# Groups of 512 tokens instead of 256 in a fused lightning-attention and MLP kernel

## The chip, the cores and the metric

The kernel runs on one core of a Trainium2 chip. Times are device microseconds. A kernel's reported time is the median of several executions; a profile is taken of one of these executions (for the kernel before, of one more), and its span is 1.7 to 1.9 us shorter than the time of that execution (2.3 us in e10). The kernel before takes 732.7 us.

The engines are called as the profile does: PE is TensorE (PEld its weight loads), DVE is VectorE, ACT is ScalarE, POOL is GpSimd, SP issues the loads and stores.

## The reference

Attention with decay over 64-token blocks, then an MLP with leaky ReLU:

```python
# q, k, v: (4, 8, 768, 64) float32; lam: (8,)
for b in range(nb):                                  # per block, per head
    intra = einsum('bhic,bhjc->bhij', qb, kb) * Dmask
    intra = einsum('bhij,bhjd->bhid', intra, vb)
    inter = einsum('bhid,bhde->bhie', qb * lam_pow, kv_state)
    out[:, :, sl] = intra + inter
    kv_state = lam_block * kv_state + einsum('bhsd,bhse->bhde', kb * rev_pow, vb)
x = out.transpose(0, 2, 1, 3).reshape(3072, 512)
h = x @ w_in                                         # 512 -> 2048, weights stored as float64
g = maximum(0.01 * h, h)
return g @ w_out                                     # 2048 -> 512
```

The kernel handles attention in 24 chunks of 128 tokens, one "step" of the program per chunk.

## The kernel before

Three parts matter: the products, the conversion of the weights, and the schedule.

**Products.** Each matrix product is done with seven block products instead of eight. Operands are quadrants A11 to A22 and sums of them, S1 to S4; the weights have B11 to B22 and differences T1 to T4. The seven products of a unit run in the order P1, P2, P6, P5, P7, P3, P4, into two kinds of PSUM bank: Z (two of them) and W (one). P6, P7 and P4 add onto Z, where P1 left its result, so P1's result has to be copied out ("keep 0") before P6 may add onto it:

```python
return [lambda: (mult("Z", "P1", ins("P1"), True), keep(0, "Z")),
        lambda: (mult("W", "P2", ["tot1"] + ins("P2"), True), total(0, "W")),
        lambda: (mult("Z", "P6", ["keep0"] + ins("P6")), keep(1, "Z")),
        lambda: (mult("W", "P5", ["tot0"] + ins("P5"), True), keep(3, "W")),
        ...]
```

`keep` is a copy of a product's result on ScalarE, except in a down unit (the second matrix product) that adds to an earlier unit's result. There it is an addition into the output tile `os` on VectorE. An up unit (the first matrix product) ends with the sums S1, S2, S3 of its results on VectorE, which the down unit needs, and the down unit adds S4 after P2. The sums of the attention's output x (tile `xs`) run on POOL:

```python
for o, a, b, op in (("S1", "A21", "A22", ALU.add), ("S2", "S1", "A11", ALU.subtract),
                    ("S3", "A11", "A21", ALU.subtract), ("S4", "A12", "S2", ALU.subtract)):
    if o in names:
        e = nc.vector if eng == "DVE" else nc.gpsimd
        run(eng, us, lambda: e.tensor_tensor(t[o], t[a], t[b], op=op), after, ("sum", eng, o))
```

A group is 256 tokens, so a quadrant holds C = 128 tokens. A unit holds UP = 4 pairs of feature blocks:

```python
# up                                                  # down
for i in range(UP):                                   for i in range(UP):
    for kk in range(2):                                   nc.tensor.matmul(t, lhsT=G[..][:, i*C:(i+1)*C],
        nc.tensor.matmul(t[:, i*C:(i+1)*C],                   rhs=WO[UP*u + i][:, SO[sb], :], ...)
            lhsT=w[:, kk, :], rhs=x[:, kk, :], ...)
```

**Conversion.** A weight block arrives as float64 words and is made float32 by three ScalarE instructions and, on VectorE, a clamp, a shift and an integer addition of 512 columns each. After two blocks of a pair, four differences T1 to T4 run on POOL.

**Schedule.** The program emits instructions in an order found with its own clocks per engine: nine attention steps first, then units with one attention step in most up units.

## Time and profile before

| | kernel before |
|---|---|
| reported time | 732.7 us |
| span of the profiled execution | 731.2 us |
| TensorE busy | 709.6 us |
| first up product starts | 59.0 us |
| TensorE idle before it, after it | 17.4 us, 4.2 us |

The page and the order of time are read in the prediction. One view more, each engine's busy time in a stretch, splits the span at the first product. The columns are: stretch, its length, busy us (and instructions) of PE, PEld, DVE, ACT and POOL, the granted clock, the DMA share, GB/s.

```profile
0.00:58.99 58.99, 41.56 (x536) 34.78 (x537) 45.19 (x71) 38.06 (x62) 38.49 (x47) 0.97 0.96 250
58.99:731.20 672.21, 667.99 (x5098) 617.61 (x5096) 242.34 (x396) 184.12 (x323) 121.66 (x138) 1.00 0.15 42
```

Length less PE's busy time is idle TensorE time: 17.4 us ahead of the first product, 4.2 us in all the rest.

### The profile page before, as it was taken

The page shows a single profiled execution, that of the slowest core. Times are in us where ns is not written, and L with a number is a line of the kernel's source. Part 1 is how long each engine was busy: PE and PEld are TensorE (multiplying, and loading weights), DVE is VectorE, ACT ScalarE, POOL GpSimd, SP SyncE. Part 2 cuts the span into 40 slices and gives each one's busy share as a digit, 9 for nine tenths or more (in the row PEclk, how much of TensorE's full clock was granted, in tenths as well). Part 3 has the DMA queues.
Part 4 walks back from the last instruction along what each step waited for, and adds up shares of the span by engine and source line. Part 5 has one row for each costly group of instructions (what it writes and reads, how often), then busy time and mean ns, then how long its engine had stood idle before and what let it go on. Part 6 is the DMA issues. An engine that isn't in the chain of part 4 may idle for free.

```text
span 731.2 us, 12969 instructions
## 1 busy us (share of the span) xinstructions
PE 709.6 (97%) x5632; PEld 652.4 (89%) x5632; DVE 287.5 (39%) x466; ACT 222.2 (30%) x385; POOL 160.2 (22%) x184
## 2 busy tenths in 40 slices
PE   5779999999999999999999999999999999999998
PEld 4668988999999999989999999899899899999997
DVE  5888996724313223222321332321321323123213
ACT  4777875611312222123022131121122122111211
POOL 2879766513103102003011110200100001001000
PEclk9999999999999999999999999999999999999999
DMA  8999635302111011110210200000000000000000
GB/s 217 268 256 268 203 108 168 87 30 58 29 30 45 30 44 44 44 30 13 62 45 1 73 1 1 2 30 1 12 18 1 30 1 1 30 1 0 30 1 29
DMA packets 89289, 42.78 MB, mean 59 GB/s; under 512 B 75920, under 2 KB 84112, under 8 KB 89232
## 3 DMA queue, kind: packets, MB, share of 16 engines
q1 hardware_dynamic: 89088, 41.95, 20.8%
q8 instruction: 44, 0.72, 0.4%
q14 instruction: 13, 0.11, 0.0%
q10 hardware_dynamic: 144, 0.00, 0.0%
HBM read 35.66 MB, written 6.29 MB: 57 GB/s over the span
## 4 chain that ended last, share of the span: by engine, by line
PE 92%; DVE 4%; ACT 2%; issue 1%; DMA 1%; SPq 0%; DVEq 0%; ACTq 0%
PE Z L502 24%; PE Z L527 22%; PE W L502 18%; PE W L527 16%; PE ps L352 3%; PE pt L328 3%; PE po L415 3%; PE po L372 2%; PE pu L401 2%; DVE gS L476 1%; DMA k<-in_k_dram 1%; DVE sc L358 1%; DVE wi L278 0%; DVE wo L283 0%; DVE wi L274 0%
## 5 line engine op out<-in xcount | busy, mean ns | idle before, releaser
L527 PE MATMUL Z<-wo,gA 128*128 128x256 f32 x552 | 131.9, 382 | 0.0
L527 PEld LDWEIGHTS Z<-wo,gA 128*128 128x128 f32 x552 | 103.0, 190 | 15.5 <-issue 2.4
L502 PE MATMUL W<-xs,wi 128*128 128x128 f32 x768 | 95.2, 277 | 0.0
L502 PE MATMUL Z<-x,wi 128*128 128x128 f32 x768 | 93.7, 275 | 0.0
L502 PE MATMUL Z<-xs,wi 128*128 128x128 f32 x768 | 93.7, 275 | 0.0
L502 PEld LDWEIGHTS Z<-x,wi 128*128 128x128 f32 x768 | 91.3, 192 | 1.5 <-issue 0.3
L502 PEld LDWEIGHTS W<-xs,wi 128*128 128x128 f32 x768 | 89.5, 192 | 2.0 <-issue 0.2
L502 PEld LDWEIGHTS Z<-xs,wi 128*128 128x128 f32 x768 | 89.6, 192 | 0.1
L527 PE MATMUL W<-wo,gA 128*128 128x256 f32 x368 | 86.9, 379 | 0.0
L455 DVE TENSOR_TENSOR gA<-gA,W 128x512 f32<-128x512 f32 x46 | 31.7, 688 | 129.8 <-PE W L502 129.8
L451 ACT COPY gA<-Z 128x512 f32<-128x512 f32 x46 | 27.0, 586 | 173.0 <-PE Z L502 173.0
L527 PEld LDWEIGHTS W<-wo,gA 128*128 128x128 f32 x368 | 69.8, 190 | 9.5
L467 ACT ACTIVATE gA<-gA 128x512 f32<-128x512 f32 x69 | 43.4, 629 | 112.2 <-DVE gA L455 112.1
L381 POOL TENSOR_TENSOR k<-k,decay 128x512 f32<-128x512 f32 x20 | 23.3, 1163 | 210.2 <-PE pt L328 210.2
L476 POOL TENSOR_TENSOR xs<-x 128x256 f32<-128x256 f32 x28 | 23.3, 831 | 191.5 <-PE W L502 191.5
L502 PE MATMUL W<-x,wi 128*128 128x128 f32 x384 | 46.8, 275 | 0.0
L455 DVE TENSOR_TENSOR gA<-gA,Z 128x512 f32<-128x512 f32 x23 | 15.8, 688 | 76.2 <-PE Z L502 76.2
L502 PEld LDWEIGHTS W<-x,wi 128*128 128x128 f32 x384 | 44.8, 192 | 0.0
L527 PE MATMUL Z<-wo,gS 128*128 128x256 f32 x184 | 44.0, 382 | 0.3
L527 PE MATMUL W<-wo,gS 128*128 128x256 f32 x184 | 43.6, 380 | 0.0
L358 DVE TENSOR_TENSOR sc<-ps,decay 128x512 f32<-128x512 f32 x48 | 30.9, 685 | 31.3 <-PE ps L352 31.3
L527 PEld LDWEIGHTS Z<-wo,gS 128*128 128x128 f32 x184 | 34.5, 190 | 6.8 <-DVE os L449 1.9
(77 smaller groups left out, 782.6 us busy)
## 6 DMA issues: line engine op xcount, KB each, us to landing
ws<-in_moe_w_in_dram SPq DMA_DIRECT2D x16, 512.0 KB, 5.5
ws<-in_moe_w_out_dram SPq DMA_DIRECT2D x16, 512.0 KB, 4.8
k<-in_k_dram SPq DMA_DIRECT2D x24, 256.0 KB, 4.0
q<-in_q_dram SPq DMA_DIRECT2D x24, 256.0 KB, 4.4
v<-in_v_dram SPq DMA_DIRECT2D x24, 256.0 KB, 4.6
out_dram<-os SPq DMA_DIRECT2D x24, 256.0 KB, 2.0
lam_b<-in_lam_dram ACTq DMA_DIRECT2D x1, 4.0 KB, 3.9
```

The lines of the kernel that those rows point to most:

```text
L328: nc.tensor.transpose(out=pt[:, hp, :], in_=pair(loaded[c][i], hp), identity=ident)
L352: nc.tensor.matmul(ps[hi][:, hp, :], lhsT=kT[b][HALF[hi], hp, :], rhs=qT[b][HALF[hi], hp, :], start=(hp == 0), stop=True, skip_group_check ...
L358: run("DVE", 0.72, lambda: nc.vector.tensor_tensor(sc[b][:, hi], ps[hi], decay[:, hi], op=ALU.mult), ["ps"], ("sc", b))
L372: nc.tensor.matmul(po[b][HALF[hi], hp, :], lhsT=state[(b - 1) % 2][HALF[hi], hp, :], rhs=qsT[b][HALF[hi], hp, :], start=(hp == 0), stop=False,
L381: run("POOL", 1.2, lambda: nc.gpsimd.tensor_tensor(kr, kr, _bc(pow_k, 3, D), op=ALU.mult), [("pt", "k")], ("kd", a))
L415: nc.tensor.matmul(po[b][HALF[hi], hp, :], lhsT=tv[:, 2 * hp + hi, :], rhs=sc[b][:, hi, hp, :], start=(not inter and hp == 0), stop=True, ...
L451: run("ACT", 0.6 if long else 0.38, lambda: nc.scalar.copy(dst(i), st[tag]), [tag], f"keep{i}")
L455: lambda: nc.vector.tensor_tensor(dst(i), dst(i), st[tag], op=ALU.add), [f"keep{i}", tag], f"tot{i}")
L467: run("ACT", 0.64, lambda: nc.scalar.activation(out=dst, in_=src, func=AF.Prelu, bias=0.0, scale=1.0, alpha=0.01), [after], gives)
L476: run(eng, us, lambda: e.tensor_tensor(t[o], t[a], t[b], op=op), after, ("sum", eng, o))
L502: nc.tensor.matmul(t[:, i * C:(i + 1) * C], lhsT=w[:, kk, :], rhs=x[:, kk, :], start=(first and i == 0 and kk == 0), stop=(i == UP - 1 and ...
L527: nc.tensor.matmul(t, lhsT=G[g, u][sa][:, i * C:(i + 1) * C], rhs=WO[UP * u + i][:, SO[sb], :], start=(first and i == 0), stop=(i == UP - ...
```

## The change

Its intent: matmuls that move 256 columns also in up products, a smaller first unit so that products start earlier, fewer and wider instructions on VectorE for the conversion, and some of the weights' differences on VectorE.

```diff
-    NG = NCH // 2
+    GC = 4
+    NG = NCH // GC
+    T = GC * C // 2          # 256 tokens in a quadrant
-    UP = 4
+    UP = 2
-    NX = 6
-    NF = 2
+    NX = 3
+    WARM = 10
...
+    idle = pp.tile([P, 2 * P], F32, name="idle", tag="W")
+    for _ in range(WARM):
+        nc.tensor.transpose(out=idle[:, 0:P], in_=ident, identity=ident)
...
+    T_DVE = [0, 3, 4, 6, 11, 13, 14]
+    FIRST, STEPS = 5, [1, 0, 0, 2, 2, 2, 1, 1, 0, 0, 1, 0, 0, 0, 0, 2]
...
         def clamp():
-            nc.vector.tensor_scalar(dest(), dest(), HI_MIN, HI_MAX, op0=ALU.max, op1=ALU.min)
+            d = W[p][:, 0:4, :].rearrange("p a b -> p (a b)")      # 1024 columns; the shift too
+            nc.vector.tensor_scalar(d, d, HI_MIN, HI_MAX, op0=ALU.max, op1=ALU.min)
...
-            for o, x, y in (("T1", "B12", "B11"), ("T2", "B22", "T1"), ("T3", "B22", "B12"), ("T4", "B21", "T2")):
-                later["POOL"].append((yes, 0.9, part(o, x, y), [("w", n)], (o, n)))
+        eng, e = ("DVE", nc.vector) if n // 2 in T_DVE else ("POOL", nc.gpsimd)
+        for o, x, y, m in (("T1", "B12", "B11", 2), ("T2", "B22", "T1", 1), ("T4", "B21", "T2", 1)):
+            ...                                                    # T1 and T3 in one, m = 2
...
-                sums("POOL", 0.8, ...x quadrants..., A[4:], [("x", 2 * g + 1)])
+                sums("DVE" if g == 0 else "POOL", ..., A[4:], [("x", GC * g + GC - 1)])
...
# up
-                    nc.tensor.matmul(t[:, i * C:(i + 1) * C], lhsT=w[:, kk, :], rhs=x[:, kk, :],
+                    nc.tensor.matmul(t[:, i, :], lhsT=w[:, kk, :], rhs=x[:, kk, :],       # 256 columns
# down
-            for i in range(UP):
-                nc.tensor.matmul(t, lhsT=G[g, u][sa][:, i * C:(i + 1) * C], rhs=WO[...], ...)
+            for m in range(T // P):
+                for i in range(UP):
+                    nc.tensor.matmul(t[:, m, :], lhsT=G[g, u][sa][:, i, m * P:(m + 1) * P], rhs=WO[...], ...)
```

Cuts are marked by "...". Not shown are the new order of loads, the bookkeeping of staging rooms, and the output tile, which is now a whole group's and written in four parts.

More of the change, by code (lines that the diff above doesn't have):

```diff
@@ L78 @@
     NCH = B * NCB
-    NG = NCH // 2
+    GC = 4
+    NG = NCH // GC
+    T = GC * C // 2
     NP = FO // 2
     HD = d_model // 2
-    UP = 4
+    UP = 2
     NU = NP // UP
-    NX = 6
-    NF = 2
+    NX = 3
+    WARM = 10
     HALF = (slice(0, D), slice(D, 2 * D))
-    assert D == 64 and KO == HP == 4 and S % C == 0 and NCH % 2 == 0 and NP % UP == 0
+    assert D == 64 and KO == HP == 4 and S % C == 0 and NCH % GC == 0 and NP % UP == 0
     const = ctx.enter_context(tc.tile_pool(name="const", bufs=1))
@@ L140 @@
     NW = len(blocks)
-    ROOMS = [f"{w}{p}" for w in ("wi", "wo") for p in range(UP, NP)]
-    ROOMS[-2:-2] = ["st0", "st1"]
-    ROOMS_G = ROOMS[-2:]
-    LOADS = "wccwcwcwwcwccwwwwcwwcwwcwwcwwwwwwwwwwwwwwww" + "c" * NCH
-    SLACK, AHEAD = 0.4, 6.0
-    PLAN = [('a', 0, 0, 9), ('i', 0, 0, 1), ('i', 1, 0, 1), ('o', 0, 0, 1), ('o', 1, 0, 0)]
-    PLAN += [(w, g, u, w == "i") for g in range(NG) for u in range(g < NF, NU) for w in "io"]
-    busy = set(ROOMS_G)
+    ROOMS = ["st"] + [f"{w}{p}" for w, p, h in reversed(blocks) if h == 0 and p >= UP]
+    LOADS = "ccwwcwcccwcwwwwcwwwwwccwwwwwwcwwwwwwwwwwwww" + "c" * NCH
+    SLACK, AHEAD = 0.7, (8.0, 16.0)
+    T_DVE = [0, 3, 4, 6, 11, 13, 14]
+    FIRST, STEPS = 5, [1, 0, 0, 2, 2, 2, 1, 1, 0, 0, 1, 0, 0, 0, 0, 2]
     rooms = {}
@@ L197, in pump @@
     def pump(urgent=False):
-        while urgent or clk["DMA"] < clk["PE"] + AHEAD:
+        while urgent or clk["DMA"] < clk["PE"] + AHEAD[fin > 3]:
             able = [x for x in sorted(y[0] for y in loads.values() if y) if x[2]()]
@@ L208, in load_w @@
         rooms[n] = room_free(n)
-        pool, size = (tp, 2 * d_model) if rooms[n][:2] == "st" else (wop, 7 * QB)
+        pool, size = (tp, 2 * d_model) if rooms[n] == "st" else (wop, 7 * QB)
         t = pool.tile([P, size], F32, name="ws", tag=rooms[n], bufs=1)
@@ L217, in go, with taken, conversion @@
                 nc.sync.dma_start(out=w_raw[n], in_=moe_w_out[f * P:(f + 1) * P, :])
-        run("DMA", 1.95, go, [("w", m) for m in range(n) if rooms[m] == rooms[n]], ("raw", n))
+        run("DMA", 1.95, go, [("lowp", m) for m in range(n) if rooms[m] == rooms[n]], ("raw", n))
         ready["raw", n] += 2.0
     def room_free(n):
-        later_on = {f"{w}{p}" for w, p, h in blocks[n + 1:] if (w, p) != blocks[n][:2]} | {"st0", "st1"}
-        taken = busy.union(rooms[m] for m in range(w_done, n))
-        return next((r for r in ROOMS if r in later_on and r not in taken), None)
+        later_on = {f"{w}{p}" for w, p, h in blocks[n + 1:] if (w, p) != blocks[n][:2]} | {"st"}
+        return next((r for r in ROOMS if r in later_on and r not in taken()), None)
+    def taken():
+        return {rooms[m] for m in w_raw}
     HI_MAX = _float_of(0x47EFFFFF)
     HI_MIN = _float_of(0x38100000)
-    def conversion(n):
+    def conversion(n, first):
         kind, p, h = blocks[n]
@@ L250, in may @@
         def may():
-            tag = f"{kind}{p}"
-            return n <= w_done + 2 and tag not in busy and all(rooms[m] != tag for m in range(w_done, len(rooms)))
+            return h == 1 or n <= w_done + 2 and f"{kind}{p}" not in taken()
         def magnitude():
@@ L271, in sign_part @@
             nc.scalar.activation(out=addend(BF16, 1), in_=words(1, F32), func=AF.Sign, bias=tiny[:, 0:1])
+            del w_raw[n]
         def clamp():
-            nc.vector.tensor_scalar(dest(), dest(), HI_MIN, HI_MAX, op0=ALU.max, op1=ALU.min)
+            d = W[p][:, 0:4, :].rearrange("p a b -> p (a b)")
+            nc.vector.tensor_scalar(d, d, HI_MIN, HI_MAX, op0=ALU.max, op1=ALU.min)
         def shift():
-            d = dest().bitcast(I32)
+            d = W[p][:, 0:4, :].rearrange("p a b -> p (a b)").bitcast(I32)
             nc.vector.tensor_scalar(d, d, 3, None, op0=ALU.logical_shift_left)
@@ L283, in low @@
             nc.vector.tensor_tensor(d, d, lo.pop(n).rearrange("p (a b) -> p a b", a=2), op=ALU.add)
-            del w_raw[n]
             w_done = n + 1
@@ L288, in yes, with part @@
             return True
-        def part(out, a, b):
-            return lambda: nc.gpsimd.tensor_tensor(W[p][:, s[out], :], W[p][:, s[a], :], W[p][:, s[b], :], op=ALU.subtract)
-        later["ACT"].append((may, 0.69, magnitude, [("raw", n)], ("mag", n)))
-        later["ACT"].append((lambda: n < w_done + 2, 0.69, low_part, [("raw", n)], ("lo", n)))
-        later["ACT"].append((yes, 0.69, sign_part, [("raw", n)], ("lowp", n)))
-        later["DVE"].append((yes, 0.55, clamp, [("mag", n)], ("c", n)))
-        later["DVE"].append((yes, 0.55, shift, [], ("s", n)))
-        later["DVE"].append((yes, 0.87, low, [("lowp", n)], ("w", n)))
-        if h == 1:
-            for o, x, y in (("T1", "B12", "B11"), ("T2", "B22", "T1"), ("T3", "B22", "B12"), ("T4", "B21", "T2")):
-                later["POOL"].append((yes, 0.9, part(o, x, y), [("w", n)], (o, n)))
+        def part(out, a, b, m):
+            return lambda: e.tensor_tensor(*(W[p][:, s[i]:s[i] + m, :] for i in (out, a, b)), op=ALU.subtract)
+        later["ACT"].append((may, 0.67, magnitude, [("raw", n)], ("mag", n)))
+        later["ACT"].append((lambda: h == 0 or n < w_done + 2, 0.78, low_part, [("raw", n)], ("lo", n)))
+        later["ACT"].append((yes, 0.87, sign_part, [("raw", n)], ("lowp", n)))
+        if h == 0:
+            return low
+        later["DVE"].append((yes, 0.95, clamp, [("mag", n)], ("c", n - 1)))
+        later["DVE"].append((yes, 0.95, shift, [], ("s", n - 1)))
+        later["DVE"].append((yes, 0.84, first, [("lowp", n - 1)], ("w", n - 1)))
+        later["DVE"].append((yes, 0.84, low, [("lowp", n)], ("w", n)))
+        eng, e = ("DVE", nc.vector) if n // 2 in T_DVE else ("POOL", nc.gpsimd)
+        for o, x, y, m in (("T1", "B12", "B11", 2), ("T2", "B22", "T1", 1), ("T4", "B21", "T2", 1)):
+            us = {"DVE": 0.15 + 0.27 * m, "POOL": 0.13 + 0.75 * m}[eng]
+            later[eng].append((yes, us, part(o, x, y, m), [("w", n)], (o, n)))
     loads = {"c": [], "w": []}
@@ L418, in last @@
             run("PE", 1.0, go, [("sc", b), ("v", b), ("x", b - 1)], "po")
-            g, h = b // 2, b % 2
+            g, r, t = b // GC, b % GC * C // T, b % GC * C % T
             if g not in X:
-                X[g] = xp.tile([P, 4, 2, C], F32, name="x", tag="x", bufs=NX)
+                X[g] = xp.tile([P, 2, 2, KO // 2, T], F32, name="x", tag="x", bufs=NX)
             del loaded[b]
@@ L424, in last @@
             ready["fin", b] = ready["po"]
-            x = X[g][:, 2 * h:2 * h + 2].rearrange("p a k c -> p (a k) c")
+            x = X[g][:, r, :, :, t:t + C].rearrange("p a k c -> p (a k) c")
             run("ACT", 0.6, lambda: nc.scalar.mul(x, po[b], 4.0), ["po"], ("x", b))
@@ L433, with product @@
             "P5": ("S1", "T1"), "P6": ("S2", "T2"), "P7": ("S3", "T3")}
-    def product(mm, us, cols, dst, put, done, ins, add=False):
-        long, st = cols > HD, {}
+    def product(mm, us, dst, put, done, ins, add=False):
+        st = {}
         def mult(tag, name, after, first=False):
             if first:
-                t = pp.tile([P, 2 * QB], F32, name=tag, tag=tag, bufs=2 if tag == "Z" else 1)
-                st[tag] = t[:, 0:cols]
+                st[tag] = pp.tile([P, UP, T], F32, name=tag, tag=tag, bufs=2 if tag == "Z" else 1)
             run("PE", us, lambda: mm(st[tag], name, first), after, tag)
@@ L448, in keep @@
             if add:
-                run("DVE", 0.42, lambda: nc.vector.tensor_tensor(dst(i), dst(i), st[tag], op=ALU.add), [tag], f"keep{i}")
+                run("DVE", 0.72, lambda: nc.vector.tensor_tensor(dst(i), dst(i), st[tag], op=ALU.add), [tag], f"keep{i}")
             else:
-                run("ACT", 0.6 if long else 0.38, lambda: nc.scalar.copy(dst(i), st[tag]), [tag], f"keep{i}")
+                run("ACT", 0.6, lambda: nc.scalar.copy(dst(i), st[tag]), [tag], f"keep{i}")
         def total(i, tag):
-            run("DVE", 0.72 if long else 0.42,
+            run("DVE", 0.72,
                 lambda: nc.vector.tensor_tensor(dst(i), dst(i), st[tag], op=ALU.add), [f"keep{i}", tag], f"tot{i}")
@@ L481, in begin @@
         def begin():
-            if u == 0 or g < NF:
-                xs = xp.tile([P, 4, 2, C], F32, name="xs", tag="xs")
-                if u == 0:
-                    X[g] = {s: X[g][:, i] for i, s in enumerate(A[:4])}
-                X[g].update({s: xs[:, i] for i, s in enumerate(A[4:])})
-                sums("POOL", 0.8, {s: x.rearrange("p k c -> p (k c)") for s, x in X[g].items()}, A[4:], [("x", 2 * g + 1)])
-            if u == 0 and 0 < g < NF:
-                t = [wop.tile([P, 7 * QB], F32, name="g", tag=r) for r in ROOMS_G]
-                G[g, u] = {s: t[i // 3][:, i % 3 * UP * C:(i % 3 + 1) * UP * C] for i, s in enumerate(A[:6])}
-            else:
-                G[g, u] = {s: xp.tile([P, UP * C], F32, name=f"g{s}", tag=f"g{s}")[:, :] for s in A[:6]}
+            if u == 0:
+                x = X[g]
+                xs = xp.tile([P, 4, KO // 2, T], F32, name="xs", tag="xs")
+                X[g] = {s: x[:, i // 2, i % 2] if i < 4 else xs[:, i - 4] for i, s in enumerate(A)}
+                sums("DVE" if g == 0 else "POOL", 1.8 if g else 0.72, {s: x.rearrange("p k c -> p (k c)") for s, x in X[g].items()}, A[4:],
+                     [("x", GC * g + GC - 1)])
+            G[g, u] = {s: xp.tile([P, UP, T], F32, name=f"g{s}", tag=f"g{s}") for s in A[:6]}
             G[g, u].update(S3=G[g, u]["A21"], S4=G[g, u]["A12"])
@@ L510, in done @@
                 sums("DVE", 0.72, G[g, u], ("S1", "S2", "S3"), ["A21", "A22", "A11"])
-        parts = product(mm, 1.79, UP * C, lambda i: G[g, u][q4[i]], lambda z: leaky(G[g, u]["A21"], z, "Z", "A21"), done,
-                        lambda name: [("sum", "POOL", PROD[name][0]), ("x", 2 * g + 1)])
+        parts = product(mm, 1.73, lambda i: G[g, u][q4[i]], lambda z: leaky(G[g, u]["A21"], z, "Z", "A21"), done,
+                        lambda name: [("sum", "POOL" if g else "DVE", PROD[name][0]), ("x", GC * g + GC - 1)])
         return [lambda: (begin(), parts[0]())] + parts[1:]
@@ L520, in o @@
             if g not in osb:
-                osb[g] = tp.tile([P, 2 * d_model], F32, name="os", tag="os", bufs=NF)
-            return osb[g][:, i * HD:(i + 1) * HD]
+                osb[g] = tp.tile([P, GC, d_model], F32, name="os", tag="os", bufs=1)
+            return osb[g][:, i // 2 * 2:i // 2 * 2 + 2, i % 2 * HD:(i % 2 + 1) * HD]
         def mm(t, name, first):
             sa, sb = PROD[name]
-            for i in range(UP):
-                nc.tensor.matmul(t, lhsT=G[g, u][sa][:, i * C:(i + 1) * C], rhs=WO[UP * u + i][:, SO[sb], :],
-                                 start=(first and i == 0), stop=(i == UP - 1), skip_group_check=True)
+            for m in range(T // P):
+                for i in range(UP):
+                    nc.tensor.matmul(t[:, m, :], lhsT=G[g, u][sa][:, i, m * P:(m + 1) * P], rhs=WO[UP * u + i][:, SO[sb], :],
+                                     start=(first and m == 0 and i == 0), stop=(i == UP - 1), skip_group_check=True)
             if name == "P2":
@@ L533, in put @@
             if u == 0:
-                run("ACT", 0.38, lambda: nc.scalar.copy(o(2), z), ["Z"])
+                run("ACT", 0.6, lambda: nc.scalar.copy(o(2), z), ["Z"])
             else:
-                run("DVE", 0.42, lambda: nc.vector.tensor_tensor(o(2), o(2), z, op=ALU.add), ["Z"])
+                run("DVE", 0.72, lambda: nc.vector.tensor_tensor(o(2), o(2), z, op=ALU.add), ["Z"])
         def done(i):
-            if u == NU - 1 and 0 < i < 3:
-                m0 = (2 * g + i - 1) * C
-                nc.sync.dma_start(out=out[m0:m0 + C, :], in_=osb[g][:, (i - 1) * d_model:i * d_model])
-        return product(mm, 1.73, HD, o, put, done,
+            if u == NU - 1:
+                rows = out[(g * GC + i // 2 * 2) * C:(g * GC + i // 2 * 2 + 2) * C, i % 2 * HD:(i % 2 + 1) * HD]
+                nc.sync.dma_start(out=rows.rearrange("(m p) n -> p m n", p=P), in_=o(i))
+        return product(mm, 1.73, o, put, done,
                        lambda name: [PROD[name][0], ("sum", "DVE", PROD[name][0])], u > 0)
@@ L556, in together @@
             x()
+    first = None
     for n in range(NW):
-        conversion(n)
+        first = conversion(n, first)
     for i, x in enumerate(LOADS):
@@ L568 @@
     pump()
-    for what, g, u, n in PLAN:
-        if what != "a":
-            need((2 * u + "io".index(what) + 1) * NW // 4)
-        together({"a": lambda g, u: [], "i": up, "o": down}[what](g, u), n)
-        if (what, g, u) == ("o", NF - 1, 0):
-            busy.clear()
-        pump()
+    together([], FIRST)
+    for n, (g, u, w) in enumerate((g, u, w) for g in range(NG) for u in range(NU) for w in range(2)):
+        need((2 * u + w + 1) * NW // (2 * NU))
+        together((up, down)[w](g, u), STEPS[n] if n < len(STEPS) else w == 0)
 _INS = ['q', 'k', 'v', 'lam', 'moe_w_in', 'moe_w_out']
```

## The prediction

> **What bounds the kernel now.** I read the page first: engines, then slices, then the chain that ended last.
>
> ```profile
> PE 709.6 (97%) x5632; PEld 652.4 (89%) x5632; DVE 287.5 (39%) x466; ACT 222.2 (30%) x385; POOL 160.2 (22%) x184
> ...
> PE   5779999999999999999999999999999999999998
> ...
> DVE  5888996724313223222321332321321323123213
> ...
> POOL 2879766513103102003011110200100001001000
> ...
> DMA  8999635302111011110210200000000000000000
> ...
> PE 92%; DVE 4%; ACT 2%; issue 1%; DMA 1%; SPq 0%; DVEq 0%; ACTq 0%
> ```
>
> TensorE is the bound everywhere but in the first three slices (55 us), where DMA is full and DVE and POOL are at 7 to 9 tenths. So two things can save time: a cheaper stream of products, and less of the opening. A busy matmul row is a latency, so I took the pace from the order of time on TensorE, late, without attention:
>
> ```profile
> 584.77 1.95 PE L502 MATMUL W<-xs,wi 128*128 128x128 f32 x16
> 586.56 1.95 PE L502 MATMUL Z<-xs,wi 128*128 128x128 f32 x16
> 588.35 1.95 PE L502 MATMUL W<-xs,wi 128*128 128x128 f32 x16
> ...
> 593.65 1.89 PE L527 MATMUL W<-wo,gA 128*128 128x256 f32 x8
> 595.38 1.89 PE L527 MATMUL Z<-wo,gS 128*128 128x256 f32 x8
> 597.10 1.89 PE L527 MATMUL W<-wo,gS 128*128 128x256 f32 x8
> ```
>
> Columns are start, duration, line. Start to start, an up product (16 instructions of 128 columns) takes 1.787 us, 111.7 ns each; a down product (8 of 256 columns) 1.727 us, 215.9 ns each. Same columns in all, 0.060 us less.
>
> The opening, same view:
>
> ```profile
> 46.48 0.63 PE L328 MATMUL pt<-ident,k 128*128 128x128 f32 x4 [0.75 <-DMA k<-in_k_dram]
> ...
> 58.01 1.05 PE L415 MATMUL po<-sc,v 128*64 128x128 f32 x16
> 58.99 2.05 PE L502 MATMUL Z<-x,wi 128*128 128x128 f32 x16
> ```
>
> Nine attention steps run before the first product at 59.0 us, because its unit needs eight blocks of w_in converted. The stretches 0 to 20, 20 to 40 and 40 to 60 us hold only 12.05, 14.88 and 15.64 us of TensorE work: 17.4 us idle.
>
> **What the Trainium skill says.** "TensorE: Matmul & The Clock Gate", section "Back-to-back issue gap", gives N/2.4 + 2.5 ns a warm matmul, and "FP8 and Floating Point Precision", section "TensorE Precision Notes", four passes for true fp32. Two instructions per product of tiles, so two passes each: 512 column cycles are 213.3 ns, and the trace's 215.9 leaves 2.6, which agrees. For 128 columns 106.7 leaves 5.0, twice the fixed part; so the trace says a little more than the page for short ones. "SBUF — State Buffer", section "Who interferes with whom": a VectorE instruction with two SBUF inputs, or in a two-port mode, and a GpSimd instruction reading SBUF exclude each other for a whole instruction. The trace agrees:
>
> ```profile
> 77.44 2.31 POOL L291 TENSOR_TENSOR wo<-wo 128x256 f32<-128x256 f32 x2
> 77.95 1.22 DVE L476 TENSOR_TENSOR gS<-gA,gA 128x512 f32<-128x512 f32 x1
> 79.20 1.10 DVE L476 TENSOR_TENSOR gS<-gS,gA 128x512 f32<-128x512 f32 x1
> ...
> 592.75 0.69 DVE L476 TENSOR_TENSOR gS<-gA,gA 128x512 f32<-128x512 f32 x1 [1.73 <-ACT gA L467]
> ```
>
> The same sum takes 0.69 us alone and 1.22 beside POOL.
>
> **The change, part by part.**
>
> *Matmuls.* Up products stay 24 units x 7 = 168, but run as 8 instructions of 256 columns: 168 x 0.060 = 10.1 us off the path. Down products keep 8 of 256. All 336 products then cost 336 x 1.727 = 580.3 us.
>
> *Opening.* Units of two pairs need four w_in blocks, and the instruction order shows five attention steps before the first product. The fifth waits for chunk 4's k and q. Landing in the kernel before fits 4.0 us + bytes / 0.26 MB per us: k of chunk 7 stands behind 11.0 MB and lands at 46.4 (wait above), and the first k, behind 0.79 MB, at 7.0 (measured 6.98). In the new queue order chunk 4's q ends at 4 chunks (3.15 MB), six blocks (3.15 MB), k and q (0.52): 6.8 MB, 30.2 us. Then transposes 0.5, copy 0.6, pu 0.5, po 1.0, copy of x 0.6 from their rows: the first product starts at about 33.3 us instead of 59.0. The ten warm transposes and k being first in the queue help only ahead of this DMA limit: zero.
>
> *Attention moved.* The period of an up plus a down unit is 29.6 us with a step and 24.6 without, so an interleaved step costs 5.0 us. Twenty steps now follow the first product instead of sixteen. Less the missing parts of first and last chunks of each sequence (pieces from the order of time: 1.05 and 0.55 us, and 1.0 for the last step) they come to 100 - 3.2 - 2.2 - 1.0 = 93.6 us. The same sum for before: 59.0 + 168 x (1.787 + 1.727) + 75.3 + tail 3.5 = 728.1; measured 731.2, so 3.1 us are small stalls (I saw 0.5 once and about 0.25 in many late units).
>
> *Down outputs.* VectorE's out-of-PSUM additions grow from 128x256 at 0.42 us to 128x512 at 0.69. In a late down unit S1 starts 0.83 us after the unit does, then S2, S3, an os copy, and after the second product S4 and the os addition. With the larger copies the last ends about 5.0 us in; the fourth product wants the bank at 5.2. It fits with 0.2 us to spare while POOL is silent. Tail: +0.3 us.
>
> *Conversion.* Before, 32 clamps at 0.67 and 32 shifts at 0.79 us; I put 1024 columns at about 0.9, so 16 + 16 cost 29 us instead of 47; seven pairs of differences moved to VectorE cost about 1.8 each, 13 us. VectorE breaks even but has the stretch to 160 us for it. Following its instruction order with these durations: from 33.3 us the work before the sum S2 of the first down unit is 18.2 us, needed by 54.1; for the second down unit it runs from 61 to 78.5, needed at 78.3; for the third it has 7 us to spare. I allow 2.5 us of stalls there.
>
> *Sums of x.* For groups 1 to 5 they sit on POOL, now 128x512, about 1.4 us each against 0.73 alone, and begin when the last up unit of the group has read xs, that is just before the last down unit's S1. Where no attention delays them (groups 3, 4, 5) S1, S2 and S3 alternate with POOL's instructions. Walking it: S2 ends 4.0 us into the unit instead of 2.3, and product three wants it at 3.5; the bank is free at 6.7 to 8.0 instead of 5.0. That is 1.4 to 2.9 us a boundary, 5.5 us in three.
>
> Sum: 33.3 + 580.3 + 93.6 + 3.8 = 711.0; + 2.5 + 5.5 = 719.0 us of span. Reported time is 1.8 us over the span (733.03 and 731.2): 720.8, which I round to 720.
>
> **Rivals.**
> 1. No new wait. Stalls stay near the 3 us of before: span 714, time 716, faster by 2.3%. For it: the schedule looks tuned (lists of steps and of pairs per engine), and my DVE walk has little real deficit.
> 2. VectorE becomes the bound from 33 to 160 us. It was 17.9 to 19.7 of 20 us busy from 40 to 100 us, POOL instructions get longer, so each lost lock costs up to 1.5 us. At 10% over my walk the second down unit and its neighbours wait 5 to 10 us: time 726 to 730. Against it: the second and third units have two attention steps inside, which give slack back.
> 3. The opening doesn't shrink as DMA allows. If copies on ACT or state additions on VectorE, which cost TensorE 1.3 and 1.5 us before, stand behind conversions, the first product slips to 37: time 724.
> 4. Only the matmul saving counts, the earlier start being eaten by weights arriving late: about 723 to 727. Against: blocks for the second up unit land near 50 us, needed at 62.7.
>
> **Range and chances.** Floor 711.0 + 1.8 = 713 without stalls; rival 2 gives the top: 714 to 728. The 2% line is 718.2 us, that is, at most 5.4 us of stalls in all against my 8. The schedule looks tuned and may beat my walk: faster 0.44, same 0.54, slower 0.02.
>
> **What would show it.** First up product at 33 us (off by 2: the DMA fit fails); product pitch 1.73 us in both kinds (1.79 for up: the matmul term fails); pieces with a wait on VectorE's sums or os additions at the start of the last down unit of groups 2, 3, 4, with POOL's xs work beside them (none: the lock term fails); waits on converted weights between 70 and 85 us. I am wrong above all if the opening is longer or the lock waits are absent.

## The result, and the profile after

The changed kernel takes 720.5 us (720.15 to 721.74, four executions) against 732.7 us. The ratio is 0.9835, with a 95% interval from 0.9818 to 0.9852. Ratios here are the mean time of one kernel's fast runs over that of the other's fast runs of the same rounds, so not quite the ratio of the medians quoted. At a 2% threshold this counts as the same; it is a real gain of 1.65%.

The page of the changed kernel, the lines that answer to those of before (busy time of each engine, slices in tenths, the chain that ended last):

```profile
PE 702.1 (98%) x4298; PEld 599.2 (83%) x4298; DVE 329.1 (46%) x483; ACT 218.8 (30%) x361; POOL 120.2 (17%) x111
...
PE   7899999999999999999999999999999998999997
...
DVE  5997899733333443324335333343522344324324
...
POOL 3732464314010004100104011000200003000000
...
DMA  8996446513001003401012110000100000100001
...
PE 93%; DVE 4%; issue 2%; ACT 1%; DMA 1%
```

The opening is two slices long instead of three. VectorE works more and POOL less than before. TensorE is still the bound. The product stream, in order of time on TensorE (start, duration, line), late and without attention:

```profile
644.87 1.89 PE L506 MATMUL Z<-xs,wi 128*128 128x256 f32 x8
646.60 1.89 PE L506 MATMUL W<-xs,wi 128*128 128x256 f32 x8
648.32 1.89 PE L506 MATMUL Z<-xs,wi 128*128 128x256 f32 x8
```

Start to start an up product takes 1.73 us, as a down product does. The opening in the same view; brackets hold idle time and what ended it:

```profile
30.39 0.66 PE L337 MATMUL pt<-ident,q 128*128 128x128 f32 x4 [1.02 <-DMA q<-in_q_dram]
...
32.46 1.99 PE L506 MATMUL Z<-x,wi 128*128 128x256 f32 x8
34.29 1.89 PE L506 MATMUL W<-x,wi 128*128 128x256 f32 x8
37.02 1.96 PE L506 MATMUL Z<-xs,wi 128*128 128x256 f32 x8 [0.83 <-DVE xs L484]
```

The first product starts at 32.5 us, after a wait for the load of chunk 4's q. Then the third product waits again, for VectorE's sums of x. The busy time split at the first product:

```profile
0.00:32.46 32.46, 25.16 (x290) 20.71 (x290) 23.46 (x39) 20.16 (x32) 15.76 (x22) 1.00 0.93 248
32.46:718.40 685.94, 676.99 (x4010) 578.47 (x4008) 305.65 (x445) 198.60 (x329) 104.40 (x90) 1.00 0.18 50
```

Idle TensorE time ahead of the first product fell from 17.4 to 7.3 us; after it, it rose from 4.2 to 9.0 us. Busy time fell by 7.4 us, though 2.4 us of ten extra transposes were added. So 12.8 us of span are 7.4 of work, 10.1 of idle time in the opening, less 4.7 of new idle time. (The transposes fill a part of that idle time with work of no use: without them, in e5, it is 8.6 us and not 7.3.) The list of waits of TensorE names most of the last (total us, times, longest):

```profile
PE Z L532 <- DVE os L457: 3.9, 3, 2.2
...
PE Z L506 <- DVE xs L484: 0.8, 1, 0.8
...
PE W L506 <- DVE gA L463: 0.3, 1, 0.3
```

The largest of the three waits on `os`, in order of time on three engines. It lies in the last down unit of group 4:

```profile
602.69 1.27 POOL L484 TENSOR_TENSOR xs<-xs,x 128x512 f32<-128x512 f32 x1
602.73 1.89 PE L532 MATMUL Z<-wo,gA 128*128 128x256 f32 x8
...
603.92 1.72 POOL L484 TENSOR_TENSOR xs<-x 128x512 f32<-128x512 f32 x1
...
604.54 1.64 DVE L484 TENSOR_TENSOR gS<-gS,gA 128x512 f32<-128x512 f32 x1
605.60 1.71 POOL L484 TENSOR_TENSOR xs<-x,xs 128x512 f32<-128x512 f32 x1
606.11 1.75 DVE L484 TENSOR_TENSOR gA<-gA,gA 128x512 f32<-128x512 f32 x1
607.78 0.67 DVE L457 TENSOR_TENSOR os<-os,Z 128x512 f32<-128x512 f32 x1
...
608.50 1.99 PE L532 MATMUL Z<-wo,gS 128*128 128x256 f32 x8 [2.16 <-DVE os L457]
```

Here gS<-gS,gA is S2 and gA<-gA,gA is S3. They take 1.64 and 1.75 us instead of 0.69, because POOL's sums of x take turns with them. The addition of product one's result into `os` stands behind them in VectorE's queue, and product three (the last line) may not add onto its bank until that is done. S2, which product three needs too, is ready at 606.2 us, about when the second product ends; it is the `os` addition that comes 2.3 us late.

### The profile page after: what moved, and what is told of

It is laid out like the page before. It is cut to its first block, busy times and chain, and to the rows that moved or that the text cites. A ratio compares the mean times of both kernels' runs of the same rounds, so it can differ in the third digit from the quotient of the medians.

```text
span 718.4 us, 10161 instructions
## 1 busy us (share of the span) xinstructions
PE 702.1 (98%) x4298; PEld 599.2 (83%) x4298; DVE 329.1 (46%) x483; ACT 218.8 (30%) x361; POOL 120.2 (17%) x111
## 4 chain that ended last, share of the span: by engine, by line
PE 93%; DVE 4%; issue 2%; ACT 1%; DMA 1%
PE Z L532 23%; PE Z L506 23%; PE W L506 17%; PE W L532 17%; PE pt L337 3%; PE ps L361 3%; PE po L381 2%; PE po L424 2%; PE pu L410 1%; DVE gS L484 1%; DMA k<-in_k_dram 1%; DVE xs L484 1%; DVE sc L367 0%; DVE wi L288 0%; DVE os L457 0%
## 5 line engine op out<-in xcount | busy, mean ns | idle before, releaser
L532 PE MATMUL Z<-wo,gA 128*128 128x256 f32 x576 | 137.6, 382 | 0.0
L506 PE MATMUL W<-xs,wi 128*128 128x256 f32 x384 | 92.1, 383 | 0.3 <-DVE gA L463 0.3
L506 PE MATMUL Z<-xs,wi 128*128 128x256 f32 x384 | 91.0, 380 | 0.8 <-DVE xs L484 0.8
L506 PE MATMUL Z<-x,wi 128*128 128x256 f32 x384 | 91.2, 380 | 0.0
L506 PEld LDWEIGHTS Z<-xs,wi 128*128 128x128 f32 x384 | 72.7, 190 | 11.3 <-ACT wo L260 1.2
L506 PEld LDWEIGHTS Z<-x,wi 128*128 128x128 f32 x384 | 72.5, 190 | 10.5 <-issue 0.9
L532 PEld LDWEIGHTS W<-wo,gA 128*128 128x128 f32 x384 | 72.6, 190 | 10.1
L506 PEld LDWEIGHTS W<-xs,wi 128*128 128x128 f32 x384 | 71.0, 190 | 10.6 <-DVE gA L463 0.5
L506 PE MATMUL W<-x,wi 128*128 128x256 f32 x192 | 45.4, 379 | 0.0
L463 DVE TENSOR_TENSOR os<-os,W 128x512 f32<-128x512 f32 x48 | 32.8, 683 | 23.9 <-PE W L532 23.9
L506 PEld LDWEIGHTS W<-x,wi 128*128 128x128 f32 x192 | 36.5, 190 | 5.0
```

The costliest lines, as they stand in the source:

```text
L463: lambda: nc.vector.tensor_tensor(dst(i), dst(i), st[tag], op=ALU.add), [f"keep{i}", tag], f"tot{i}")
L506: nc.tensor.matmul(t[:, i, :], lhsT=w[:, kk, :], rhs=x[:, kk, :], start=(first and i == 0 and kk == 0), stop=(i == UP - 1 and kk == 1), sk ...
L532: nc.tensor.matmul(t[:, m, :], lhsT=G[g, u][sa][:, i, m * P:(m + 1) * P], rhs=WO[UP * u + i][:, SO[sb], :], start=(first and m == 0 and i ...
```

## The experiments

The theory: (a) up products gain by their width alone; (b) the new waits come from POOL's sums of x and VectorE's sums shutting each other out, and reach TensorE through the place of the `os` addition in VectorE's queue; (c) otherwise only idle TensorE time counts, wherever it lies. The rivals: the opening alone made the gain; VectorE is short of time up to 160 us; the wait is for S2. Each experiment edits the changed kernel. The time, the ratio to the kernel before in its own rounds, and two readings from the profile:

| run | time us | ratio | third product starts | from there to the end |
|---|---|---|---|---|
| changed kernel | 720.5 | 0.9835 | 37.0 | 681.4 |
| e1 128 columns again | 730.87 | 0.9969 | 36.9 | 692.6 |
| e2 sums of x on VectorE | 714.59 | 0.9751 | 36.3 | 676.9 |
| e3 order of S3, S4 | 715.30 | 0.9756 | 37.4 | 676.5 |
| e4 sums of x in halves | 716.94 | 0.9782 | 36.1 | 678.7 |
| e5 no warm transposes | 720.04 | 0.9823 | 36.7 | 681.4 |
| e6 conversion in 512 columns | 722.57 | 0.9860 | 38.1 | 684.4 |
| e7 differences on POOL | 720.85 | 0.9830 | 37.1 | 681.5 |
| e8 nine steps first | 736.21 | 1.0043 | | |
| e9 the same, loads reordered | 737.54 | 1.0055 | | |
| e10 e2 and e3 | 714.42 | 0.9744 | 37.0 | 675.7 |
| e11 e10, scores earlier | 713.90 | 0.9732 | 36.7 | 676.4 |
| e12 e10, opening mended | 712.62 | 0.9717 | 36.1 | 675.4 |

The start of the third product varies from 36.1 to 37.4 us among runs whose openings are alike (changed kernel, e1 to e5, e7, e10), so the last column (span less that start, from one profile each) is the better measure of what happens later.

**e1: the width of the up matmuls.**

```diff
-  nc.tensor.matmul(t[:, i, :], lhsT=w[:, kk, :], rhs=x[:, kk, :], ...)
+  for c in (slice(0, T // 2), slice(T // 2, T)):
+      nc.tensor.matmul(t[:, i, c], lhsT=w[:, kk, :], rhs=x[:, kk, c], ...)
```

> The changed kernel with its up products cut back to 128 columns (16 instructions a product instead of 8), everything else kept. If the matmul term of the prediction is right, 168 products x 0.060 us = 10.1 us come back: about 730.6 us, ratio to the kernel before 0.997, up products 1.787 us start to start again, and the product stream is the bound throughout. If the gain came from the opening and the matmul width lies beside other waits, the time stays within 2 us of 720.5.

730.87 us: 10.4 us came back against 10.1 expected. Order of time on TensorE:

```profile
628.54 1.95 PE L507 MATMUL W<-x,wi 128*128 128x128 f32 x16
630.33 1.95 PE L507 MATMUL Z<-xs,wi 128*128 128x128 f32 x16
```

The pitch is 1.79 us again. The matmul term is shown, and with it that the product stream bounds the changed kernel; for the kernel before, the 4.2 us of idle time after the first product say so. That 10.4 comes so near to 10.1 is more than the run can show: in e1's profile the two products after the wait of 2.10 us in group 4 took 2.84 and 2.77 us, some 1.7 us more than in the changed kernel, and the fastest executions of both differ by 9.2 us (729.35 and 720.15). What the run doesn't part: each matmul instruction has a weight load of its own, so e1 brings back weight loads too (5642 of them against 4298), and the 0.060 us may belong to either.

**e2: sums of x of groups 1 to 5 on VectorE.**

```diff
-  sums("DVE" if g == 0 else "POOL", 1.8 if g else 0.72, ...)
+  sums("DVE", 0.72, ...)
```

> The sums of x of groups 1 to 5 on VectorE instead of GpSimd, where they stand behind the last down unit's work. Lock theory: the three waits of TensorE on the os addition at the start of the last down unit of groups 2, 3 and 4 (0.93 + 0.84 + 2.16 us, with a restart of about 0.15 each) vanish, 20 more VectorE instructions of 0.69 us cost nothing on the path: about 716 us, ratio 0.978. Rival (VectorE's own queue is too long there, GpSimd has no part in it): the waits stay or move to the first products of the next up unit, time 720 to 724.

714.59 us, 5.9 us less (4.5 from the third product on). No wait on `os` is left in the list of waits. The same place as above, S1 to S3 in order of time:

```profile
600.53 0.69 DVE L484 TENSOR_TENSOR gS<-gA,gA 128x512 f32<-128x512 f32 x1 [1.67 <-ACT gA L475]
601.25 0.69 DVE L484 TENSOR_TENSOR gS<-gS,gA 128x512 f32<-128x512 f32 x1
601.86 0.69 DVE L484 TENSOR_TENSOR gA<-gA,gA 128x512 f32<-128x512 f32 x1
```

All three take 0.69 us once POOL is silent. VectorE got 20 instructions more and TensorE waited less: VectorE was not short of time there, it was shut out.

**e3: S3 and S4 later in VectorE's queue**, for groups 1 to 5:

```diff
+  return [lambda: (ps[0](), sums("DVE", ..., ("S3",), ...)),     # after keep 0
+          lambda: (ps[1](), sums("DVE", ..., ("S4",), ...))] + ps[2:]   # after total 0
```

Only the added calls are shown; those at the old places are taken out.

> For groups 1 to 5, S3 is issued after the os addition of product one and S4 after that of product two; the sums of x stay on GpSimd. Queue-order theory (product three waits for the os addition, which stands behind S1, S2 and S3): the waits of 0.93 and 0.84 go to zero, the one of 2.16 to about 0.75 us (S2 still loses the lock twice), and the small gaps of about 0.15 us before product three in late units with u above 0 go too: about 4.5 us less, 716 us, ratio 0.978. Rival (product three waits for S2 itself, as the prediction said): the waits shrink by nothing, 720 us.

715.30 us, 5.2 us less (4.9 from the third product on). POOL still disturbs; the same place:

```profile
602.19 1.64 DVE L484 TENSOR_TENSOR gS<-gS,gA 128x512 f32<-128x512 f32 x1
...
603.75 0.68 DVE L457 TENSOR_TENSOR os<-os,Z 128x512 f32<-128x512 f32 x1
...
604.49 1.99 PE L532 MATMUL Z<-wo,gS 128*128 128x256 f32 x8 [0.50 <-DVE os L457]
```

S2 is as slow as before at 1.64 us, yet 2.16 us of wait became 0.50 and the two others vanished. So the wait was for the `os` addition behind S3. That S2 alone held product three up is refuted.

**e4: POOL's sums of x in instructions of 256 columns.**

```diff
+  for c in (slice(0, 256), slice(256, 512)):
+      e.tensor_tensor(t[o][:, c], t[a][:, c], t[b][:, c], op=op)
```

> The sums of x on GpSimd cut into instructions of 256 columns, the same work in twice as many pieces. If the two engines exclude each other for a whole instruction, VectorE loses up to 0.7 us a time instead of up to 1.3: S1, S2 and S3 end earlier, the 2.16 us wait falls to about 1 us, the other two to under 0.3 us: 2.3 us less in all, about 718 us, ratio 0.980. If they share the port's rate, only the amount of work counts and nothing changes: 720.5 us, waits as before.

716.94 us. Of the 3.6 us, 2.7 lie after the third product's start, which is the part to be compared with the 2.3 expected; the rest is an opening that came 0.9 us earlier in the profiled run. S1, S2 and S3 took 1.11, 1.10 and 1.21 us (0.95, 1.64 and 1.75 in the changed kernel), and one wait was left:

```profile
605.00 1.99 PE L538 MATMUL Z<-wo,gS 128*128 128x256 f32 x8 [1.25 <-DVE os L457]
```

The same work in shorter pieces cost VectorE less, 3.4 us instead of 4.3 for the three sums. With sharing of a rate it would have cost the same. That the two engines wait for each other's whole instructions fits; that they share a rate doesn't.

**e5: no warm transposes** (WARM and its loop taken out).

> The ten transposes at the very start taken out. The prediction gives them no worth: the first product waits for the load of chunk 4's q, and the first attention steps of the changed kernel ran at half pace in spite of them (1.1 us for four transposes until 15 us, 0.66 later). Expected 720.5 us within 1 us, ratio 0.9835, first product at 32 to 33 us. If the warm clock matters, the opening gets 1 to 3 us longer: 722 to 723 us.

720.04 us, from the third product on 681.4 us as before. They are worth nothing that can be measured, as predicted.

**e6: clamp and shift in 512 columns.**

```diff
+  for c in (slice(0, 512), slice(512, 1024)):
       d = W[p][:, 0:4, :].rearrange("p a b -> p (a b)")[:, c]
```

> Clamp and shift of the weights cut back to 512 columns an instruction, in the same places of the queues. If VectorE has slack from 40 us on, only the opening feels it: the third product, which already waits 0.8 us for the sums of x behind three pairs' conversions, waits some 0.5 to 1.5 us more: 721 to 722 us, ratio 0.985. If VectorE bounds the stretch to 160 us, 16 pairs x about 0.3 us (two fixed parts of 0.15 each) lie on the path: 725 us.

722.57 us, 2.1 us more. The third product:

```profile
38.05 3.55 PE L508 MATMUL Z<-xs,wi 128*128 128x256 f32 x8 [3.01 <-DVE xs L486]
```

It starts 1.0 us later than in the changed kernel, and after a wait of 3.0 us it runs at half pace, which costs 1.6 us more. The profiled execution was the slowest of four (724.15 us). Another 1.7 us of it lie far from the edit: after the wait of 2.15 us in group 4 two products took 3.34 and 2.27 us, while after the same wait in the changed kernel they took 1.99 and 1.89. VectorE does gate the opening; the 5 us of a VectorE that is short up to 160 us did not come. VectorE is not slow there by its own work alone. In the changed kernel POOL works beside it, and the first two sums of x took 1.76 and 0.99 us, 1.4 us more than two sums of 0.69; the wait of the third product was 0.83.

**e7: all differences of weights on POOL** (T_DVE empty).

> All sixteen pairs' differences on GpSimd, none on VectorE (the kernel's own scheduler moves some conversions with it). VectorE loses 13 us of work, GpSimd gains some 23. If VectorE is short, this is faster by some us: 717 or less. If GpSimd's longer chains (3.4 us a pair, behind the attention's work) come late for the first two units, TensorE waits 1 to 6 us more for differences: 721.5 to 727 us, ratio 0.985 to 0.992. I expect the second, 723 us.

720.85 us, no change: I missed with 723. TensorE waits 2.0 us for POOL's product of q in the fourth step, in a stretch where it would wait for loads anyway, and the third product starts at 37.1 us as before. Neither engine was short by that work, so the split of the differences neither won nor lost anything measurable.

**e8: nine attention steps first.**

```diff
-  FIRST, STEPS = 5, [1, 0, 0, 2, 2, 2, 1, 1, 0, ...]
+  FIRST, STEPS = 9, [0, 0, 0, 1, 1, 1, 1, 1, 0, ...]
```

> Nine attention steps before the first product, as in the kernel before, instead of five; four fewer follow it, with load order as the scheduler makes it. Idle-time theory: only idle TensorE time counts; the first product slips to 48 to 56 us, 4 x 5.0 = 20 us of attention leave the later stretch, so the time moves by the change of idle time ahead of the first product alone (7.3 us now, of which the ten transposes hide 2.4 more): 717 to 726 us, ratio 0.979 to 0.991. Rival (each us of earlier start is a us gained): 736 to 744 us.

736.21 us, a number that I gave to the rival, and outside what I gave for idle time. But both were worked out for a first product at 48 to 56 us, and it started at 64.6: sixteen weight blocks were issued ahead of chunk 7, and TensorE waited for it:

```profile
53.93 1.09 PE L337 MATMUL pt<-ident,k 128*128 128x128 f32 x4 [6.77 <-DMA k<-in_k_dram]
```

Ahead of the first product TensorE was idle for 18.1 us instead of 7.3, the clock granted there fell to 0.89, and 1.6 us of idle time came later. The first product came 32.1 us later than in the changed kernel. With a us for each us the time would have been near 753 us, so this rival is refuted by the run. Idle time in all rose by 12.3 us (28.6 against 16.3) and busy time by 3.4, which make up the 15.7 us of span. TensorE work ahead of the first product rose by 21.4 us, and after it fell by 18.0; my forecast failed on how late the chunks would come.

**e9: the same with fewer weights ahead of the chunks** (order of loads changed).

> Nine attention steps before the first product again, but with the loads reordered so that the ninth chunk stands behind five weight blocks instead of seventeen. By the landing fit (4.0 us + 9.4 MB / 0.26) its q lands at 40 us, so TensorE and not DMA should pace the opening: first product near 50 us with 6 to 9 us idle before it. Idle-time theory: about 720 us, within 4, ratio 0.977 to 0.988, though the first product is 18 us later than in the changed kernel. Rival (each us of earlier start is a us gained): 736 us or more.

737.54 us: missed by 17 us. The opening did as expected, with the first product at 47.9 us and 6.1 us idle before it. But the weights came too late then. The worst of three waits:

```profile
172.48 2.93 PE L532 MATMUL Z<-wo,gA 128*128 128x256 f32 x6 [8.43 <-DVE wo L288]
```

After the first product TensorE was idle for 22.8 us instead of 9.0. The first product came 15.4 us later than in the changed kernel, and the span grew by 18.3: 12.6 us of idle time in sum (28.9 against 16.3) and 5.7 us of busy time, in which products after the long waits ran at half pace (0.83 of the clock granted from 60 to 80 and from 160 to 180 us). That busy and idle time add up to the span is no test, for they always do. What the trace shows is where the time went: nothing was lost ahead of the first product, and the waits on converted weights (11.9 us for w_out, 2.1 for w_in) make up the new idle time. My forecast left out that the later units need their weights in time. The time alone is also what the rival would give (15.4 us later, 736 us), so this run doesn't refute it; e8 does. What the early start is worth by itself is not shown by either run; 10.1 us less idle time in the opening is what the traces before and after the change show.

**e10: e2 and e3 together.**

> Sums of x on VectorE and, for groups 1 to 5, S3 after the os addition of product one and S4 after that of product two: the edits of the second and third run together. The three large waits are gone with either, so the gains do not add: what the order adds to the second run is only the small gaps of about 0.15 us before product three, in some ten late units: 1.3 us. About 713.2 us, ratio 0.9733, and no wait of a down product on an os addition at all. If the gains added up it would be 709.5.

714.42 us. From the third product on it takes 675.7 us, 1.2 less than e2, as expected, by one profile each. No down product waits on an `os` addition any more. The gains do not add, because they remove the same waits. The times themselves don't tell e10 from e2: its executions run from 713.59 to 716.13 us, and the intervals of the two ratios overlap.

**e11: in the first up unit, an attention piece moved ahead of the third product.**

```diff
-  while m - len(extra) < m * (i + 1) // len(parts):
+  while m - len(extra) < m * (i + 1 + (fin == 4)) // len(parts):
```

> As the run before, and in the first up unit the scores of the attention step come before the third product instead of after it, so that 1.1 us of TensorE work lies in its wait for the sums of x (0.7 to 1.8 us in the runs so far) and the third piece of attention before the last product. If that wait is VectorE's own lateness, 0.7 to 1.2 us less: about 712.3 us, ratio 0.972. If VectorE is pushed later by the score multiplications coming earlier, nothing is gained: 713 to 714.

713.90 us, within the spread of e10. The wait at the third product fell from 1.8 to 0.6 us, but the fourth product's rose from 0.3 to 1.3 us. VectorE's lateness only moved on: inconclusive as a gain. (Its 676.4 us in the table leave out the scores, 1.1 us, that now lie ahead of the third product.)

**e12: e10 without the warm transposes, and the first sums of x ahead of a conversion in VectorE's queue.**

```diff
-  sums("DVE", 0.72, ..., A[4:], [("x", GC * g + GC - 1)])
+  sums("DVE", 0.72, ..., A[4:], [("x", GC * g + GC - 1)], fill=g > 0)   # don't emit waiting conversions first
```

> The order and sums-of-x edits together, without the ten warm transposes, and in the first up unit the sums of x are issued ahead of the last addition of the second w_out block's conversion on VectorE. If that queue position is what the third product waits for, the wait of 0.7 to 1.8 us in all runs so far goes to under 0.7 and the third product starts at 35.3 to 36.2 us instead of 36.1 to 37.4: about 713 us, ratio 0.972. If GpSimd's work on chunk 4 holds the sums up all the same, the third product starts at 36.5 to 37 and the time is that of the two edits, 714 us, 0.9744.

712.62 us (712.08 to 713.24), ratio 0.9717 with an interval from 0.9704 to 0.9730, and the output is correct. The third product:

```profile
36.07 1.97 PE L502 MATMUL Z<-xs,wi 128*128 128x256 f32 x8 [0.26 <-DVE xs L480]
```

It started at 36.1 us with a wait of 0.3, within what the queue-position theory said. The start alone is no proof, for it was 36.1 us in e4 and 36.3 in e2 without this edit. But from the first product's start to the third's it is 4.0 us here and 4.4 to 5.5 in the other runs with the old place in the queue (e6 aside, with 6.7), and the sums of x begin 0.9 us after the first product instead of 2.6 in e10. POOL still slows the second of them to 1.65 us. This version beats both kernels: 2.8% under the kernel before. Its interval lies just below that of e10 (0.9731 to 0.9758), with chips and rounds that differ.

## Why the prediction was right

The time was 720.5 us; the sum was 720.8, given as 720. The span was 718.4 against 719.0. So near a hit is in part luck: the stalls came to 8.0 us as predicted, but the two that were foreseen were smaller by some 2.3 us, and small gaps and a rest that were not foreseen made up for them. Step by step:

- **Matmuls, 10.1 us.** Right: the pitch is 1.73 us and e1 gave 10.4 back, about 1 us of which is uncertain.
- **Opening.** Right within a us: 32.5 instead of 33.3 us (its parts add up to 33.4), and the load of chunk 4's q ended the last wait ahead of the first product, at 30.4 us (30.2 said). From there it took 2.1 us instead of 3.2, since TensorE waited for neither copy. In the other runs with this opening (e1 to e5, e7, e10) the first product started at 30.6 to 32.0 us, in e1, e3, e4, e7 and e10 with no wait on that load, so the load is not the only thing that holds it. The step overlooked that the third product, not the first, is what the opening ends with: it starts at 36.1 to 38.1 us in all runs but e8 and e9, held by VectorE (e6, e12). "Zero" for the warm transposes was right (e5).
- **Attention moved and tail.** From the first product to the end of the last (32.46 to 714.39) are 681.9 us; less 580.3 and 93.6 this leaves 8.0 us of stalls, the sum predicted. The tail took 4.0 instead of 3.8 us.
- **Stalls while weights are converted, 2.5 us.** The size was 1.4 us (0.83 and 0.26, and some 0.3 for starting again), the place wrong: it was the first up unit; the second down unit didn't wait, and the waits on converted weights that I gave as a sign for 70 to 85 us are absent. Clamps and shifts cost 27.6 us (29 said), the moved differences 12.7 (13 said).
- **Sums of x, 5.5 us.** The mechanism was right, and so were the three units; the wait named was wrong. I had product three wait for S2 at 4.0 us and then product four for its bank at 6.7 to 8.0. In the worst unit S2 came at 3.5, product three waited for the `os` addition until 5.7, and product four didn't wait (e3). The three waits came to 3.9 us, with about 0.1 each for starting again.
- **"It fits with 0.2 us to spare".** Wrong: I had looked at product four only. For product three, the `os` addition of product one behind S3 has nothing to spare even with POOL silent, and six late units lose about 0.15 us each. They are gone in e10.
- Of the 8.0 us, 5.0 are waits on the list, about 0.5 their restarts and 0.9 to 1.2 the small gaps (six of 0.15, or e2 less e10). Some 1.5 us I can't place; an error of the attention sum is as likely as a stall.

Of the rivals, VectorE as a bound (2), an opening that doesn't shrink (3) and weights that come too late for the early start (4) didn't happen; TensorE waited for no converted weight. Rival 1, no new wait, is nearly what e10 and e12 made of it. What the early start is worth by itself stays open: e8 shows that it is not a us for each us, but both runs that moved the start moved the loads too (e8, e9).

## What to carry to other kernels

When an engine's queue is in order, look at what stands between an instruction and the consumer that waits for it; moving S3 behind the `os` addition gave as much here as removing the disturbance (676.5 and 676.9 us from the third product on). Work that is free on an idle engine can cost on a busy one: POOL's sums were cheap by themselves, but VectorE paid up to 1.1 us for an instruction that met one. And look for the idle time that an earlier start removes, not for the us by which it is earlier; here it depended on loads for both the start and what follows.

## What the Trainium skill lacked or had wrong

- "SBUF — State Buffer", section "Who interferes with whom", says that the engine that issues first holds the shared pair for a whole instruction. It doesn't say what happens when both have more to do: here they took turns, one instruction each. VectorE's sums took 1.64 and 1.75 us instead of 0.69, POOL's 1.72 and 1.71 instead of 1.27; with POOL's instructions halved VectorE's took 1.10 and 1.21 us.
- "TensorE: Matmul & The Clock Gate", section "Back-to-back issue gap", gives N/2.4 + 2.5 ns for a single matmul, and says that this is too low at small N in a stream with weight loads; the section has no figure for fp32. For fp32 in two instructions of two passes each, 256 columns left 2.6 ns a matmul instruction over the columns, but 128 columns left 5.0 (111.7 less 106.7).
